# Idle products ahead of the feed-forward part, own PSUM banks for its two halves of rows, and one strided copy for each half

## The chip, the cores and the metric

One core of one Trainium2 chip. The metric is the device time of one execution in microseconds (us). A profile's own times count from the first instruction and end some 1.8 us lower than the device time.

Each run is labelled fast or slow; for one core, slow means no more than "over 1.5% above the fastest run of the same kernel". In the traces TensorE's granted clock is 0.50 or 1.00 and changes only at edges of a grid of 3.41 us. I compare all runs of the same rounds, and give the ratio of the fast ones beside that.

## The reference

A gated linear attention (RWKV) over `[4, 8, 768, 48]`, then a mixture of experts with soft slots over its 3072 rows of 384:

```python
# attention, for each step t
cur = u * k_t (x) v_t;  y_t = r_t . (state + cur);  state = w * state + k_t (x) v_t
# soft experts: 8 experts, 4 slots each, F = 1024
logits = x @ phi                                  # [3072, 32]
slot_input = softmax(logits, axis=0).T @ x        # [32, 384]
for e in range(8):
    slot_out[e] = relu(slot_input[e] @ w1[e]) @ w2[e]
out = softmax(logits, axis=1) @ slot_out
```

## The kernel before

Twelve blocks of 256 rows go through attention and the routing sums; GpSimd meanwhile issues the loads of the experts' weights. Behind the loop come the last routing, the feed-forward part (32 slots, all experts, on column strips of the array) and the output. The parts that matter:

```python
    hT = cst.tile([P, 2, nF, P], bf, name="hT")
    nc.gpsimd.memset(hT[:], 0.0)                      # at the start
    # ...
        ones_t = cst.tile([P, ES + 16], f32, name="ones_t")[:, 0:ES]
        nc.vector.tensor_reduce(ones_t, ident[:].rearrange("p (g t) -> p t g", g=G), ...)   # cut
        nc.vector.tensor_copy(idrep[:], ones_t[:, None, :].to_broadcast([P, G, ES]))
    # ...
        W_AT = [1] * 9 + [32] * 5                     # weight loads issued after each block
        for n in range(nS):                           # nS = 12; cut to the order on TensorE
            att(n, 0); disp(n - 2, s_now); trans(n + 1, "rr"); att(n, 1)
            # ... y_open, inter, state; trans(n + 1, "kk"); rowsum; xt(n - 1); intra(n); lg(n - 1)
            load_w(W_AT[n])
        disp(nS - 2, s_now)
        last_routing(nS - 1)
        disp(nS - 1, s_now)
        # ... csum_r, unsiT on DVE
        lexp_t(nG - 1)                                # transpose on PE, copy on ACT
        rowsum(nG - 1)
    # ...
        def up(x):
            h_p = ffn_ps.tile([P, 2, F // 2], f32, name=f"h_p{x}")      # both halves, one tile
            h_s[x] = ffn.tile([P, 2, F // 2], bf, name="h_s")
            for fh in range(2):
                for mi in range(nM):
                    for c in range(XE):
                        nc.tensor.matmul(h_p[c * ES:(c + 1) * ES, fh, :], unsiT[:, mi, :],
                                         w1_all[:, x * XE + c, mi, fh * (F // 2):(fh + 1) * (F // 2)],
                                         start=(mi == 0), stop=(mi == nM - 1), tile_position=(0, c * ES),
                                         skip_group_check=True)
                # relu of this half: DVE for fh == 0, ACT for fh == 1
        def turn(x):
            # per half: four transposes into hT_p, then
                for c in range(XE):
                    o = c * ES + (x * XE + c) * Spe
                    eng = nc.vector.tensor_copy if c % 2 == 0 else nc.scalar.copy
                    eng(hT[:, x, sl, o:o + Spe], hT_p[:, :, o:o + Spe])
        up(0); up(1); turn(0); down(0); turn(1); down(1)
```

The softmax here doesn't subtract the row's maximum and nothing guards it: scores larger than these inputs give would overflow.

## Time and profile before

| | value |
|---|---|
| time, median of 4 runs | 143.39 us (142.93 to 144.71) |
| span of the profile | 141.2 us |
| PE, DVE, ACT, POOL busy | 69%, 72%, 55%, 56% |
| feed-forward part in the profile | 109.74 to 123.99 us |
| last packet of the weight queue | 116.66 us |

The page's row of the granted TensorE clock, one digit for each fortieth of the span (3.5 us), 9 for full and 5 for half:

```profile
PEclk9999999995996986999757978999655555995555
```

From slice 29 (counted from 0) the row reads 5: the clock is at half through the last routing and the up products, and full only for slices 34 and 35.

### The profile page before, as it was taken

Reading aid. Unit: us, or ns where it says so; the run is one execution under the profiler, and the core shown is the slowest. Engines: PE = TensorE matmul, PEld = TensorE weight load, DVE = VectorE, ACT = ScalarE, POOL = GpSimd, SP = SyncE. Lnnn points to the kernel's source line nnn. Section 1 sums busy time; section 2 is a strip of 40 time slices with the busy share of each in tenths; the row PEclk is TensorE's granted clock in tenths of the full one; section 3 lists DMA queues with packets and bytes.
Section 4 is the critical chain, followed back from the end, with each engine's and each line's share of the span. In section 5 each row is a group of like instructions: output and inputs, shape, how many; then the busy total and the mean of one; then the engine's idle time right before and its main releaser. Section 6 shows DMA issues by size and latency. Waiting matters only on the chain.

```text
span 141.2 us, 4091 instructions
## 1 busy us (share of the span) xinstructions
PE 97.7 (69%) x1715; PEld 67.9 (48%) x1715; DVE 101.7 (72%) x198; ACT 77.5 (55%) x136; POOL 79.0 (56%) x63
## 2 busy tenths in 40 slices
PE   0826496769759869685898857786866679959200
PEld 0325284658557556564577645664454226623000
DVE  7899998999796888889986878989633211169510
ACT  4839466676775584949583766858033013128510
POOL 7309999999998749595895939995000000000000
PEclk9999999995996986999757978999655555995555
DMA  2999997999999999999999999999999990009994
GB/s 34 323 325 322 325 324 167 188 287 235 265 216 276 223 232 253 203 202 289 211 263 235 208 299 186 194 197 210 204 205 203 204 148 0 5 0 358 411 404 168
DMA packets 51351, 31.78 MB, mean 225 GB/s; under 512 B 38386, under 2 KB 46836, under 8 KB 51332
## 3 DMA queue, kind: packets, MB, share of 16 engines
q0 software_dynamic: 11600, 12.63, 54.2%
q1 hardware_dynamic: 39316, 18.88, 46.7%
q8 instruction: 13, 0.21, 0.5%
q10 hardware_dynamic: 416, 0.00, 0.2%
q14 instruction: 6, 0.05, 0.1%
HBM read 39.38 MB, written 4.72 MB: 312 GB/s over the span
## 4 chain that ended last, share of the span: by engine, by line
PE 37%; DVE 32%; ACT 17%; DMA 5%; issue 4%; POOL 0%; DVEq 0%; ACTq 0%; POOLq 0%
DVE at_s L292 14%; PE at_p L287 7%; ACT t_kk L272 5%; DMA out_dram<-o_s 5%; ACT v_bf L219 4%; PE h_p L535 4%; DVE k_l L238 4%; PE so_p L561 4%; ACT xt_s L381 4%; PE s_p L332 3%; PE t_p L269 3%; PE xl_p L379 3%; ACT rp L232 2%; PE xl_p L416 2%; PE y_p L314 2%
## 5 line engine op out<-in xcount | busy, mean ns | idle before, releaser
L292 DVE TENSOR_TENSOR at_s<-at_p,mask 128x512 bf16<-128x512 f32 x48 | 30.9, 685 | 7.9 <-PE at_p L287 7.8
L209 POOL TENSOR_TENSOR rr<-r_l,W_n 128x768 bf16<-128x768 f32 x11 | 20.0, 1817 | 16.3 <-DMA r_l<-in_r_dram 16.2
L211 POOL TENSOR_TENSOR kk<-k_l,W_k 128x768 bf16<-128x768 f32 x11 | 20.6, 1875 | 0.4 <-PE s_p L332 0.4
L212 POOL TENSOR_TENSOR k_l<-k_l,u_rep 128x768 f32<-128x768 f32 x11 | 20.0, 1814 | 0.9
L232 ACT COPY rp<-r_l 128x384 f32<-128x384 f32 x23 | 11.2, 486 | 14.4 <-DVE k_l L238 12.7
L287 PE MATMUL at_p<-t_rr,t_kk 64*64 64x128 bf16 x384 | 14.7, 250 | 6.1 <-DVE at_s L292 4.8
L272 ACT COPY t_rr<-t_p 128x1024 bf16<-128x1024 bf16 x11 | 11.1, 1012 | 9.7 <-PE t_p L269 9.6
L171 POOL DMA_DIRECT2D w_all<-in_moe_w_dram x19 | 15.6, 831 | 1.3 <-DMA w_all<-in_moe_w_dram 1.3
L287 PEld LDWEIGHTS <-t_kk 64*64 64x64 bf16 x384 | 9.0, 121 | 9.6 <-issue 7.7
L272 ACT COPY t_kk<-t_p 128x1024 bf16<-128x1024 bf16 x12 | 12.1, 1005 | 2.8 <-PE t_p L269 2.6
L238 DVE TENSOR_TENSOR k_l<-k_l,rp 128x384 f32<-128x384 f32 x23 | 12.6, 549 | 0.8
L341 DVE TENSOR_TENSOR st<-s_p,wm 128x384 bf16<-128x384 f32 x20 | 11.0, 552 | 1.9 <-PE s_p L332 1.9
L332 PE MATMUL s_p<-v_bf,kk 64*128 64x96 bf16 x160 | 12.4, 229 | 0.0
L256 DVE TENSOR_TENSOR dv<-v_bf,rp 128x768 bf16<-128x768 bf16 x12 | 11.4, 953 | 1.2
L249 DVE TENSOR_REDUCE rp<-k_l 128x16 f32<-128x768 f32 x12 | 11.5, 958 | 0.3
L332 PEld LDWEIGHTS <-kk 64*128 64x128 bf16 x160 | 9.0, 107 | 5.3 <-issue 5.3
L269 PE MATMUL t_p<-ident,kk 128*128 128x128 bf16 x96 | 9.1, 251 | 3.1 <-DVE kk L205 3.1
L381 ACT COPY xt_s<-xl_p 128x768 bf16<-128x768 bf16 x11 | 8.8, 800 | 3.6 <-PE xl_p L379 3.6
L365 ACT CAST x_t<-y_p 128x768 bf16<-128x768 f32 x11 | 8.9, 806 | 2.8 <-PE y_p L354 2.8
L219 ACT CAST v_bf<-v_l 128x768 bf16<-128x768 f32 x12 | 9.9, 828 | 0.0
L314 PE MATMUL y_p<-st,t_rr 128*128 128x96 bf16 x80 | 8.2, 236 | 2.3 <-DVE st L341 2.3
L598 ACT ACTIVATE o_s<-o_p,rsum_r 128x384 f32<-128x384 f32 x12 | 6.4, 585 | 5.9 <-PE o_p L590 3.7
(103 smaller groups left out, 180.9 us busy)
## 6 DMA issues: line engine op xcount, KB each, us to landing
w_all<-in_moe_w_dram POOLq DMA_DIRECT2D x15, 768.0 KB, 9.6
k_l<-in_k_dram SPq DMA_DIRECT2D x12, 384.0 KB, 10.2
r_l<-in_r_dram SPq DMA_DIRECT2D x12, 384.0 KB, 9.2
v_l<-in_v_dram SPq DMA_DIRECT2D x12, 384.0 KB, 9.2
out_dram<-o_s SPq DMA_DIRECT2D x11, 384.0 KB, 4.1
w_all<-in_moe_w_dram POOLq DMA_DIRECT2D x4, 192.0 KB, 19.6
out_dram<-o_s SPq DMA_DIRECT2D x2, 192.0 KB, 1.9
phi_f<-in_moe_phi_dram POOLq DMA_DIRECT2D x1, 48.0 KB, 4.7
```

The costliest lines, as they stand in the source:

```text
L171: nc.gpsimd.dma_start(out=dst, in_=src)
L209: nc.gpsimd.tensor_mul(rr[:, :, :, 0:D], jh(r_l), W_n[:])
L211: nc.gpsimd.tensor_mul(kk[:, :, :, 0:D], jh(k_l), W_k[:])
L212: nc.gpsimd.tensor_mul(ku, ku, u_b)
L219: nc.scalar.copy(v_bf[:], jh(loads[n][2]))
L232: nc.scalar.copy(rp[:], jh(loads[n][0])[:, j, :, :])
L238: nc.vector.tensor_mul(s["ku"][:, j, :, :], s["ku"][:, j, :, :], s["rps"][j][:])
L272: nc.scalar.copy(t_s[:], t_p[:])
L287: nc.tensor.matmul(at_p[a][g * HF:(g + 1) * HF, q, :], kT[sl, q, g, j, :], rT[sl, q, g, :, :].rearrange("p j c -> p (j c)"), start=True, s ...
L292: nc.vector.tensor_mul(s["at"][:, a, j, :, :], at_p[a][:], mask[:, j, None, :].to_broadcast([P, nP, P]))
L332: nc.tensor.matmul(s_p[:, q * D2:(q + 1) * D2], s["kk"][sl, j, 2 * q:2 * q + 2, :].rearrange("p h d -> p (h d)"), s["v"][sl, j, 2 * q:2 * ...
L381: nc.scalar.copy(xt_s[:], xl_p[:, 0:XW])
```

## The change

Its intent: keep the array's clock up into the feed-forward part with products whose result nobody reads, and take away the waits inside that part. It also moves hT's memset from the start to a late block and builds `idrep` in another way, since one copy for a half now needs each expert's slots at the same offset of its strip. The diff, cut (...):

```diff
     hT = cst.tile([P, 2, nF, P], bf, name="hT")
-    nc.gpsimd.memset(hT[:], 0.0)
...
-    unsiT = cst.tile([P, nM, ES], bf, name="unsiT")
+    unsiT = cst.tile([P, nM, 2, ES], bf, name="unsiT")
...
-        ones_t = cst.tile([P, ES + 16], f32, name="ones_t")[:, 0:ES]
-        nc.vector.tensor_reduce(ones_t, ident[:].rearrange("p (g t) -> p t g", g=G),
-                                axis=mybir.AxisListType.X, op=ALU.add)
-        nc.vector.tensor_copy(idrep[:], ones_t[:, None, :].to_broadcast([P, G, ES]))
+        nc.vector.memset(idrep[:], 0.0)
+        for c in range(XE):
+            nc.vector.tensor_copy(idrep[c * ES:(c + 1) * ES, :, c * Spe:ES], ...)
...
+        def fill(count):
+            pad = ps.tile([P, H, D], f32, name="pad", tag="rp")
+            for _ in range(count):
+                nc.tensor.matmul(pad[:].rearrange("p h d -> p (h d)"), ident[:], w1_all[:, 0, 0, 0:Dm],
+                                 start=True, stop=True, skip_group_check=True)
...
             trans(n + 1, "rr")
+            if n == nS - 1:
+                fill(2)
...
             trans(n + 1, "kk")
+            if n == nS - 1:
+                fill(2)
...
             load_w(W_AT[n])
+            if n == nS - 3:
+                nc.gpsimd.memset(hT[:], 0.0)
+        fill(2)
         disp(nS - 2, s_now)
         last_routing(nS - 1)          # with fill(2) between its transposes and its products
         disp(nS - 1, s_now)
+        fill(4)
...
-            h_p = ffn_ps.tile([P, 2, F // 2], f32, name=f"h_p{x}")
+            h_p = [ffn_ps.tile([P, F // 2], f32, name=f"h_p{x}{fh}") for fh in range(2)]
...
-                for c in range(XE):
-                    o = c * ES + (x * XE + c) * Spe
-                    sl = slice(fh * (nF // 2), (fh + 1) * (nF // 2))
-                    eng = nc.vector.tensor_copy if c % 2 == 0 else nc.scalar.copy
-                    eng(hT[:, x, sl, o:o + Spe], hT_p[:, :, o:o + Spe])
+                own = slice(x * XE * Spe, x * XE * Spe + Spe)
+                eng = nc.vector.tensor_copy if fh == 0 else nc.scalar.copy
+                eng(hT[:, x, sl, :].rearrange("p f (c t) -> p f c t", c=XE)[:, :, :, own],
+                    hT_p[:].rearrange("p f (c t) -> p f c t", c=XE)[:, :, :, own])
```

I call the two tiles of `h_p` "own banks": no trace shows the banks. The fills come to twelve products of 128x128 by 384 columns. Two of the expectations below say fourteen; that was a miscount of mine.

## The prediction

> **What bounds the kernel now.** I read the chain of work that ended last first, because no engine is busy throughout (DVE 72%, PE 69% of a 141.2 us span). Its lines behind the loop:

> ```profile
> 109.74 1.49 PE h_p L535 x12
> 111.26 0.70 DVE h_s L540
> 112.00 2.77 PE h_p L535 x24
> 114.80 0.70 DVE h_s L540
> 115.55 1.47 PE h_p L535 x12
> 117.02 0.97 PE hT_p L550 x8
> 117.99 2.84 PE so_p L561 x32
> 120.82 0.55 PE hT_p L550 x8
> 121.41 2.56 PE so_p L561 x31
> ```

> The feed-forward part runs from 109.74 to 123.99: 14.25 us, one engine after the other. Twice TensorE stops for the relu of the first half of rows, though the next product needs only the other half: both halves lie in one tile. Two equal batches of 32 down products take 2.84 and 2.56 us, yet the second has 16 steps (a group of three strips, then one) and the first 8. The clock explains that. I found its edges by narrow windows; they lie 3.41 us apart, so I read windows on that grid (columns: length, busy PE, PEld, DVE, ACT, POOL, then granted clock, DMA share, GB/s):

> ```profile
> 92.99:96.41 3.42, 3.05 (x72) 2.40 (x72) 3.30 (x6) 2.42 (x5) 3.42 (x5) 1.00 1.09 196
> 96.41:99.82 3.41, 1.50 (x49) 1.23 (x46) 3.21 (x6) 1.92 (x4) 0.96 (x2) 1.00 1.11 210
> 99.82:103.23 3.41, 2.88 (x39) 1.76 (x28) 1.94 (x4) 0.27 (x1) 0.00 (x0) 0.50 1.30 203
> ...
> 110.06:113.47 3.41, 2.62 (x28) 1.00 (x24) 0.69 (x1) 0.00 (x0) 0.00 (x0) 0.50 1.31 201
> 113.47:116.89 3.42, 2.63 (x26) 0.65 (x16) 0.69 (x1) 0.60 (x1) 0.00 (x0) 0.50 0.82 125
> 116.89:120.30 3.41, 3.41 (x39) 2.64 (x39) 0.57 (x4) 1.19 (x5) 0.00 (x0) 0.50 0.02 5
> 120.30:123.71 3.41, 3.37 (x50) 1.92 (x42) 0.57 (x4) 0.59 (x4) 0.00 (x0) 1.00 0.00 0
> ```

> A window with 1.50 us of PE work cost the clock; 2.62 and 2.63 did not bring it back; 3.41 did. Over the whole trace a full clock fell after windows of 1.45 to 2.20 us and mostly stayed from 2.19 up; a half clock rose after 3.32 us or more and not after 3.22. So keeping needs about 65% and regaining about 97%.

> Last I read the timeline of the start, because the diff moves a memset from there:

> ```profile
> 2.08 2.70 DVE L115 TENSOR_SCALAR mask<-col_f,row 128x128 bf16<-128x128 f32 x2
> 2.80 1.82 POOL L126 MEMSET hT<- 128x2048 bf16 x1
> ...
> 10.39 1.89 POOL L209 TENSOR_TENSOR rr<-r_l,W_n 128x768 bf16<-128x768 f32 x1 [5.77 <-DMA r_l<-in_r_dram]
> 10.54 2.56 DVE L207 TENSOR_TENSOR k_l<-k_l,u_rep 128x768 f32<-128x768 f32 x1
> ...
> 12.25 2.52 POOL L211 TENSOR_TENSOR kk<-k_l,W_k 128x768 bf16<-128x768 f32 x1
> ```

> Two mask instructions of 128 columns end at 4.78, just behind the memset's end at 4.62. The product at 10.54 takes 2.56 us where its neighbours of 768 columns take 0.95; it ends 0.8 us behind GpSimd's product, which started 0.15 us earlier. Both DVE delays are on the chain.

> [...]

> **The change part by part.**

> (1) hT's memset leaves the start (not the headline, but I give it weight). The masks [...] end near 3.1, 1.65 us earlier. The DVE queue reaches u_rep at 6.2 instead of 7.8, but u_rep needs a product that PE ends at 6.71: 6.75, a gain of 1.05. The idrep work there was two instructions; it becomes five. With DVE starts some 0.15 us apart I put its cost at +0.2, so kk starts at 7.97 instead of 8.80, and the disputed product at 9.71 instead of 10.54. Now DVE is ahead of GpSimd, whose operand lands at 10.39: the product takes 0.95, ends at 10.66, and what followed at 13.20 starts near 10.7. TensorE's operands through ACT shift by 0.83 only, so the first masking at 15.12 comes near 12.7. GpSimd's k times u for the next block, done at 16.65, would end near 16.1, and DVE's product that needs it (18.38) can't start earlier: that leaves 2.2 us. Later blocks have 3 to 6 us between GpSimd and its reader, so 2.2 us should live through the loop. At its new place, behind the last weight issue at 98.64, the memset has until about 117: free.

> (2) Own banks for the halves: the two gaps vanish, 111.22 to 112.00 and 114.77 to 115.55, 0.79 each, together 1.6 us. PE's h_p work at half clock is then 12 steps of 512 columns at 0.427 = 5.1 us.

> (3) One copy for each half instead of four small ones that alternated between DVE and ACT: 16 become 4. The small ones took 0.17 us each with some 0.05 between, but ran beside the down products; only about 0.3 us of the first batch was exposed (2.84 against 8 steps of 0.32 = 2.56). Gain 0.3, less near 0.1 of new waiting. The reciprocal product doubles to 192 columns: +0.1, hidden behind the row sums.

> (4) The clock. A continuous feed-forward part at half clock is 5.1 up + 0.9 turn + 2.6 down + 0.9 turn + 5.1 down = 14.6 us; at full clock 7.3, and 7.5 with short waits. Without gaps it regains the clock by itself at the first edge behind a filled window: 3.1 to 6.5 us in, mean 4.8 (counting 0.3 of row-sum work directly ahead). Total 7.5 + 4.8/2 = 9.9 instead of 14.25: 4.35 us gained, which holds (2) and (3).

> (5) The fills, if the clock has already fallen. One costs what an equal product (L327) takes in the chain: 0.16 at full, 0.32 at half. Before the second att: mostly in a gap, 0 to 0.3. Before the row sums: 0.64 with a wait for DVE behind it that stays; +0.35. Before the dispatch: in a gap of 1.02, nothing. In the last routing: +0.27. Four ahead of the last Lexp transpose: 1.28 of PE time ahead of the transpose, ACT copy and row sums, which queue in front of the up products; less what h_p waited for the reciprocal in its old shared tile, +1.05. Sum 1.7 us later.

> Sum at half clock on entry: 2.2 + 4.35 - 1.7 = 4.85 us, thus 138.2. If the fills hold the clock, they cost some 0.3 in all and the feed-forward part lasts 7.5; but the last expert's weights land in pieces up to 116.66 (my sum over the software queue's packets; the window 116.89:120.30 shows 5 GB/s), and the last group needs them. So the end of the down products can't come much before 117, against 123.99: 7 us, thus 136.1.

> **The rivals.** (a) The fills keep the clock. For: one added at 98.7 lies in the poor window. Against: 1.50 + 0.32 is still under 2.2 us, and some 3.4 us window always finds this trough. I give 30%: 136. (b) The clock is down, fills only cost, the gapless part regains it: 70%, 138.2, with 0.9 either way from the phase. (c) The start gains nothing, because DVE still comes behind GpSimd at 10.39 or the loop waits for loads: 15%, adds 2.2 in either case, 140.3 for (b). For: the DMA queues are near full throughout. Against: loop chain pieces are DVE, ACT and PE, with POOL 0%. (d) Weight landings become the bound: only together with (a), a floor of 136.

> **Range and chances.** 0.7 x 138.2 + 0.3 x 136.1 = 137.6, plus 0.15 x 2.2 = 137.9 us. Phase gives 0.9, the loop's own throttled windows (six of half clock, some 0.6 us each by comparing block times of 7.2 and 8.4 to 9 us) another 1: 80% between 135.7 and 140.2. Faster by over 2% means under 140.2: 0.88; within 2%: 0.11; slower: 0.01.

> **What would show it.** Masks ending near 3.1 and the k times u product at 0.95 us; the first masking near 12.7; the last block's first masking near 96 instead of 98.26. No relu between the batches of h_p. The feed-forward part near 10 us at half clock on entry, or near 8 with PEclk at 1.00 before it. If the start is unmoved, step (1) is wrong; if the up products run at half clock to their end, the fills were only cost; if the last down group waits for DMA, (d) is at work. A clock that never rises in the feed-forward part would make the whole prediction wrong, near 142.

## The result, and the profile after

The changed kernel took 138.09 us at the median of 4 runs (135.43 to 139.65), against 143.39. The ratio of fast runs is 0.9475, interval 0.9341 to 0.9609: faster. (Ratios here are the mean time of one kernel's fast runs over that of the other's of the same rounds, so not quite the ratio of the medians.) Two later calls ran it again: all 16 runs lie between 134.83 and 139.87, mean 137.34.

The first profile fell on a run of 139.48, in the upper part of the spread. Its row of the clock, and its chain behind the routing (start, length, engine, tile, line):

```profile
PEclk9999999999855699869757977999755557999755
```

```profile
110.27 5.21 PE h_p L552 x48
115.49 0.34 PE hT_p L567 x4
115.92 0.20 DVE hT L571
116.17 1.48 PE so_p L578 x32
117.65 0.34 PE hT_p L567 x4
118.02 0.20 DVE hT L571
118.27 2.16 PE so_p L578 x32
```

The row has 5 from slice 29 again (counted from 0); it rises in slice 33, is full in slices 34 to 36 and falls in 37. All 48 up products are one piece; no relu stands between them. The part lasts 10.18 us, from 110.27 to the cast at 120.45, where it lasted 14.25. But it *begins* 0.53 us later than before, although the loop had come 1.39 us earlier to its last block (first masking at 96.87 against 98.26): the fills cost 1.9 us here. Its windows on the clock's grid show that they bought nothing in this run (length, PE busy, PEld, DVE, ACT, POOL, clock, DMA share, GB/s):

```profile
94.80:98.21 3.41, 1.55 (x38) 0.91 (x38) 2.94 (x6) 1.87 (x4) 0.85 (x2) 1.00 1.11 207
98.21:101.63 3.42, 3.42 (x35) 1.74 (x34) 1.98 (x4) 0.27 (x1) 2.38 (x2) 0.50 1.22 203
101.63:105.04 3.41, 3.06 (x55) 2.33 (x55) 0.74 (x2) 0.99 (x2) 0.00 (x0) 0.50 1.31 203
105.04:108.45 3.41, 2.87 (x34) 2.00 (x33) 1.12 (x4) 1.20 (x5) 0.00 (x0) 0.50 1.32 205
108.45:111.87 3.42, 2.71 (x24) 1.15 (x26) 0.79 (x4) 0.27 (x1) 0.00 (x0) 0.50 1.31 202
111.87:115.28 3.41, 3.41 (x36) 1.25 (x28) 1.30 (x2) 0.60 (x1) 0.00 (x0) 0.50 1.18 181
```

The clock fell at 98.21 and rose only at 115.28, 5.0 us into the feed-forward part. The second line is the surprise: PE is busy for the whole window and the clock stays at half. By the prediction's rule (97% busy regains it) it had to rise at 101.63.

The same kernel in a fast run, traced with the experiments (135.63 us, from e11):

```profile
99.04:102.46 3.42, 3.07 (x28) 1.94 (x26) 1.21 (x3) 0.00 (x0) 0.07 (x1) 0.50 1.31 203
102.46:105.87 3.41, 3.04 (x60) 2.22 (x58) 1.13 (x3) 1.40 (x3) 0.00 (x0) 0.50 1.32 204
105.87:109.28 3.41, 2.47 (x33) 1.50 (x35) 1.25 (x5) 1.11 (x4) 0.00 (x0) 1.00 1.31 204
```

```profile
108.86 2.77 PE h_p L552 x48
112.32 1.49 PE so_p L578 x32
114.41 2.16 PE so_p L578 x32
```

Here a window with 3.04 us of PE work brought the clock back at 105.87, 3 us ahead of the up products, which then take 2.77 instead of 5.21; the whole part lasts 7.74 us. A third trace (e4, 134.83 us) had the clock full from 94.0 on and never lost it before the output. So this kernel ran in all three ways: held, regained ahead of the feed-forward part, regained inside it.

The start, which answers to the last fence of the prediction:

```profile
2.07 0.75 DVE L115 TENSOR_SCALAR mask<-col_f,row 128x128 bf16<-128x128 f32 x2
7.48 0.76 DVE L193 COPY idrep<-ident 32x128 bf16<-32x128 bf16 x4
10.02 0.95 DVE L207 TENSOR_TENSOR k_l<-k_l,u_rep 128x768 f32<-128x768 f32 x1
10.46 2.17 POOL L209 TENSOR_TENSOR rr<-r_l,W_n 128x768 bf16<-128x768 f32 x1 [7.66 <-DMA r_l<-in_r_dram]
13.02 1.29 DVE L292 TENSOR_TENSOR at_s<-at_p,mask 128x512 bf16<-128x512 f32 x2
```

The masks end at 2.82: 0.75 us for the two, where they took 2.70. The product with u starts 0.44 us ahead of GpSimd's and takes 0.95 us; before, it started 0.15 us behind and took 2.56. Now GpSimd's product is the longer one (2.17 us, with a median of 1.82 for its eleven of this form). The prediction takes the order of the two starts for the cause; these two traces show one pair each and do not isolate it.

### What the clock answers to

The busy time failed as a measure, so I counted the work. From the timelines of eleven traces (before, changed, e1 to e6, e9 to e11) I took each 3.41 us window on the grid, and summed for all products in it: count x columns x (rows x columns of the tile) / (128 x 128). That is columns of the full array. A product of 384 columns on the full array takes 0.16 us at full clock in these traces (0.66 for four fills in e4 and e11), so a window has room for about 8,190 of them at full clock and half of that at half (an estimate from these two numbers). Over 306 windows that end before 118 us, one limit tells whether the next window has the full clock, whatever the present clock: about 3,000 columns. Limits of 2,950 to 3,050 misjudge 13 to 17 of the 306. A single limit on busy time misjudges 90 at best, and two limits, one for each clock, 39. The rows count too: with columns x width of the tile alone the best limit misjudges 39, with columns alone 75. Transposes are in the sum: they run at both clocks (128 columns start 107 ns apart at half and 56 ns at full, in the changed kernel's profile), and without them the best limit misjudges 79. It is a rule read off these traces, not a mechanism that I tested alone; window edges and missing matmul records make it inexact.

It fits most of the lines above. The fully busy window of the changed kernel held 2,757 columns, many of its products being tiles of 64x64 or of few columns; the three behind it 2,908, 3,039 and 2,576; the one that regained the clock 3,953. (The 3,039 is one of the misjudged, if the limit is 3,000. A recount that splits a product between two windows by its time gives 2,782, 2,931, 3,076, 2,707 and 4,139 for these five, so one window's count is good to some 25 to 190 columns. The number of misjudged windows stays at 13.) In the fast run, 2,585 did not and 3,211 did. A fill is 384 columns, an eighth of the limit, for 0.16 us at full or 0.32 at half clock (e4's four take 0.66, two in e5 at half clock 0.64): dense work for its time. Before the change the windows from 99.82 to 116.89 held 2,081, 2,363, 1,384, 2,789 and 2,597.

### The profile page after: what moved, and what is told of

It reads as the page before. It is cut to its first block, busy times and chain, and to the rows that moved or that the text cites.

```text
span 137.7 us, 4106 instructions
## 1 busy us (share of the span) xinstructions
PE 98.7 (72%) x1727; PEld 67.7 (49%) x1727; DVE 98.0 (71%) x195; ACT 76.8 (56%) x130; POOL 78.6 (57%) x63
## 4 chain that ended last, share of the span: by engine, by line
PE 39%; DVE 26%; ACT 19%; issue 5%; DMA 5%; POOL 0%; DVEq 0%; ACTq 0%; POOLq 0%
DVE at_s L292 14%; PE at_p L287 7%; ACT t_kk L272 5%; DMA out_dram<-o_s 5%; ACT v_bf L219 4%; DVE k_l L238 4%; PE h_p L552 4%; PE t_p L269 4%; PE s_p L332 4%; ACT xt_s L381 3%; PE xl_p L379 3%; PE so_p L578 3%; ACT rp L232 2%; PE y_p L314 2%; DVE dv L256 2%
## 5 line engine op out<-in xcount | busy, mean ns | idle before, releaser
L209 POOL TENSOR_TENSOR rr<-r_l,W_n 128x768 bf16<-128x768 f32 x11 | 20.3, 1847 | 17.7 <-DMA r_l<-in_r_dram 17.6
L211 POOL TENSOR_TENSOR kk<-k_l,W_k 128x768 bf16<-128x768 f32 x11 | 20.0, 1814 | 0.0
L354 PE MATMUL y_p<-v_bf,at_s 64*128 64x48 bf16 x384 | 9.6, 192 | 0.0
```

Of the source, the lines that this page charges most:

```text
L209: nc.gpsimd.tensor_mul(rr[:, :, :, 0:D], jh(r_l), W_n[:])
L211: nc.gpsimd.tensor_mul(kk[:, :, :, 0:D], jh(k_l), W_k[:])
```

## The experiments

"Against before" is the difference of the means of all runs of the same rounds; with standard deviations of 0.4 to 2.1 us for one run, such a difference has a standard error of some 0.4 to 0.9 us. All gave the right result.

| run | kernel | mean (lowest to highest) | against before | ratio of fast runs |
|---|---|---|---|---|
| e1 | before, memset moved | 141.44 (139.23 to 144.00) | -1.3 | 0.9901 |
| e2 | changed, no fills | 137.24 (136.44 to 138.04) | -5.5 | 0.9744 |
| e3 | changed, memset at the start | 138.50 (136.82 to 141.75) | -4.2 | 0.9773 |
| e4 | changed | 137.57 (134.83 to 139.87) | -5.1 | 0.9604 |
| e5 | before, fills only | 138.87 (137.63 to 141.01) | -3.1 | 0.9809 |
| e6 | changed, no fills, shared tile | 140.36 (137.70 to 143.43) | -1.6 | 0.9792 |
| e7 | changed, no fills, weights early | 145.84 (143.18 to 147.91) | +3.9 | 1.0189 |
| e8 | changed, weights early | 145.74 (142.60 to 147.57) | +3.8 | 1.0142 |
| e9 | changed, shared tile | 138.08 (135.04 to 141.35) | -3.5 | none (one fast run) |
| e10 | changed, no fills | 137.66 (136.96 to 138.09) | -3.9 | 0.9738 |
| e11 | changed | 136.79 (135.41 to 138.19) | -4.8 | 0.9633 |
| e12 | changed, no fills, sixth block's weights | 140.18 (137.06 to 141.86) | -1.4 | 0.9739 |

The theory at the outset was the prediction's: the start gives 2 us, the gapless part regains the clock by itself, and the fills cost what they don't repay unless they keep the clock. The rivals: the fills are what brings the clock; the start is lost again; the weights set the end.

### e1: only the memset

```diff
-    nc.gpsimd.memset(hT[:], 0.0)
...
             load_w(W_AT[n])
+            if n == nS - 3:
+                nc.gpsimd.memset(hT[:], 0.0)
```

> The kernel before with one thing changed: hT's memset moves behind the last weight issue. Theory (start): the masks end near 2.8 us instead of 4.78, the k-times-u product takes 0.95 us, the first masking starts near 12.9 instead of 15.12, and the whole run is 1.4 to 2.2 us shorter than before (ratio 0.985 to 0.990). Rival (the loop waits for loads, or the clock gives it back): the start moves in the trace but the time stays within 0.5 us of before.

Measured: first masking at 12.48 us, ratio 0.9901 with interval 0.9812 to 0.999 (unclear at 2%), mean 1.3 us below before. The start moved by 2.6 us and about half reached the end. It leans to the theory; the size is not sharp.

### e2 and e10: no fills

```diff
         def fill(count):
+            return
```

> The changed kernel with all 14 idle products left out. Theory (fills only cost while the clock is down, the gapless feed-forward part regains it by itself): the feed-forward part begins near 108.5 in the trace, 1.5 to 1.9 us earlier than with fills, still regains the clock 3 to 7 us in, and the time is 1 to 2 us shorter than the changed kernel's median of 138.1, thus near 136.5. Rival (the fills keep or regain the clock in part of the runs): slower than the changed kernel by 0.5 us or more, without its fast runs of 135.4.

> The changed kernel without fills once more, for more runs. Theory (with own banks and one copy for each half, the fills are worth nothing on average: they cost what they win, and the landing of the last weights near 117 caps the best cases): mean within 0.7 us of the changed kernel in the same rounds, and a smaller spread (no runs under 136, none over 138.5). Rival (fills still help by 1 us or more, and the earlier runs were chance): mean 1 us or more above the changed kernel.

Measured: means 137.24 and 137.66, against 137.57 and 136.79 for the changed kernel in the same rounds (e4, e11): the fills are worth -0.3 to +0.9 us, 0.3 on average, inside the noise. All twelve runs lie between 136.44 and 138.09: a spread of 1.7 us, against 5.0 with the fills. The fast runs alone favour the fills by 1.4 and 1.1 points of ratio (some 2 and 1.5 us). I put that down to the spread: all twelve runs without fills count as fast, but only two of six (e4) and four of six (e11) with them, so these are picked from the lower end. That is an argument and not an experiment; by the fast runs alone the fills would be worth having. As the theory said, the feed-forward part starts early (107.13 in e2) and regains the clock by itself, 2.7 us in (3.3 in e10). What neither theory of e2 had: it then waits. The down products of e2 (start, length, ..., idle before, and what ended it):

```profile
113.96 1.48 PE L579 MATMUL so_p<-w_all,hT 128*32 128x384 bf16 x26
115.86 0.48 PE L579 MATMUL so_p<-w_all,hT 128*32 128x384 bf16 x2 [0.42 <-DMA w_all<-in_moe_w_dram]
116.83 0.48 PE L579 MATMUL so_p<-w_all,hT 128*32 128x384 bf16 x2 [0.49 <-DMA w_all<-in_moe_w_dram]
118.04 0.48 PE L579 MATMUL so_p<-w_all,hT 128*32 128x384 bf16 x2 [0.72 <-DMA w_all<-in_moe_w_dram]
```

The last expert's four pieces of weights arrive one by one, the last packet at 117.57, and the products follow each. e10 waits once, for the last piece (0.21 us; last packet 118.2). This is the bound that the prediction gave only to the best case of the fills; both traces without fills and with own banks reach it. Whether it also makes the narrow spread is not shown.

The bound is not a fixed time. In the eleven traces with the loads as they were, the last packet ends between 114.9 (e4) and 118.3 us (e9), and always 30.4 to 32.1 us after GpSimd starts the last batch of weight loads behind the tenth block (83.5 us in e4, 86.0 in e2, 87.8 in e10). In e2 and e10 the chain of work that ended last runs from that start through GpSimd and the last load to the last down products. So a faster loop should move the bound too; that was not tested alone.

### e3: the memset back at the start

```diff
     hT = cst.tile([P, 2, nF, P], bf, name="hT")
+    nc.gpsimd.memset(hT[:], 0.0)
...
-            if n == nS - 3:
-                nc.gpsimd.memset(hT[:], 0.0)
```

> The changed kernel with hT's memset put back at the start. Theory (start): masks blocked again until about 4.7 us, and 1.4 to 2.2 us slower than the changed kernel. Rival (the start is worth nothing by the end): same time as the changed kernel within 0.5 us.

Measured: first masking at 15.65 us, mean 0.9 us above e4, with a standard error of 1.1: no more than a hint. (The ratios of the fast runs differ by 1.7 points, some 2.5 us, but e4 has only two fast runs.) Pooled over the traces it is clearer. The first masking of the last block comes at 98.26, 98.33 and 98.92 where the memset is at the start (before, e5, e3), and at a mean of 96.87 (94.64 to 97.95) in the eight traces where it is moved and the loads are as they were (changed, e1, e2, e4, e6, e9, e10, e11). So 1.6 of 2.1 us live through the loop. At the end the means leave about 1 us (e1, e3), which with errors of 0.8 and 1.1 us can't be told from 1.6.

### e4 and e11: the changed kernel again

> The changed kernel itself, unchanged, for its spread in the same rounds as the other three. Theory (the phase of the clock windows decides): times spread over 135.4 to 139.7 again, in no fixed order, longer where the mean granted clock is lower. Rival (two fixed states of the chip): two clusters with nothing between.

> The changed kernel itself, beside the other three of this call. Theory: mean 137 to 138.3, wide spread of some 135 to 140 as the clock windows fall. Rival (a slow or fast state of one chip): all six runs at one end of that.

Measured: 134.83 to 139.87 and 135.41 to 138.19, with no gap between clusters, as expected. Their traces, described above, differ in where the clock fell and rose (full from 94.0 on in e4, back at 105.87 in e11); that this makes the spread was not tested.

### e5: the fills alone

> The kernel before plus the 14 idle products at the places of the change, nothing else. Theory (the fills are a cost of 1 to 1.7 us while the clock is down, and the two relu waits in the shared tile still keep every window under 97%): 0.5 to 1.7 us slower than before, ratio 1.003 to 1.012. Rival (the fills are what keeps or regains the clock): 1.5 us or more faster than before, with the clock at 1.00 in the up products of the trace.

The diff is the `fill` lines of the change, put into the kernel before. Measured: 3.1 us faster than before (ratio of the fast runs 0.9809, interval 0.9742 to 0.9877, so clear of noise on both counts). **Here my theory fell** and its rival won: the fills are no mere cost. The windows of e5, again on the grid:

```profile
103.40:106.81 3.41, 2.85 (x53) 2.10 (x53) 0.69 (x2) 1.40 (x3) 0.00 (x0) 0.50 1.32 204
106.81:110.23 3.42, 3.25 (x35) 2.13 (x34) 1.54 (x5) 0.79 (x3) 0.00 (x0) 0.50 1.32 204
110.23:113.64 3.41, 1.91 (x30) 0.93 (x32) 0.88 (x2) 0.27 (x1) 0.00 (x0) 1.00 1.32 203
```

The window with the last routing's fills and the four behind the dispatch holds 3,584 columns (the one before it 2,904), and the clock rises at 110.23, ahead of the up products at 111.38. The relu waits in the shared tile are still there (0.79 us each), and the window that contains them (1.91 us busy, some 2,980 columns) just kept the clock.

### e6 and e9: the shared tile, without and with fills

```diff
-            h_p = [ffn_ps.tile([P, F // 2], f32, name=f"h_p{x}{fh}") for fh in range(2)]
+            h_p = ffn_ps.tile([P, 2, F // 2], f32, name=f"h_p{x}")
```

(Cut: the lines that index `h_p` follow, and e6 also leaves the fills out.)

> The changed kernel without fills and with the two halves of rows in one tile again. Theory (own banks give 1.6 us directly and let the clock rise some 3 us earlier): 3 to 4 us slower than the same kernel with own banks (137.1), near 140.5; the two waits of 0.79 us are back in the chain and the clock rises only behind the up products. Rival (the landing of the last weights near 117 sets the end in any case): within 1.5 us of 137.1.

> The changed kernel with its fills, but the two halves of rows in one tile again: the fourth corner of fills by tiles. Theory (fills and own banks are two ways to the same thing, a clock that rises at or before the feed-forward part; either one alone gives most of it): between 137.5 and 139, thus at most 1.3 us slower than the changed kernel in the same rounds, though the same edit without fills cost 3 us. Rival (the two gains add): 3 us slower than the changed kernel, near 140.7.

Measured, as differences to before in the same rounds:

| | no fills | fills |
|---|---|---|
| shared tile | -1.6 (e6) | -3.5 (e9) |
| own banks | -5.5, -3.9 (e2, e10) | -5.1, -4.8 (e4, e11) |

By these means own banks are worth 2.3 to 3.9 us without fills (3.1 on average) and 1.3 to 1.6 with them; fills are worth 1.9 on the shared tile (3.1 in e5) and about nothing on own banks. Each seems to replace much of the other. The sizes are not settled: the error is near 1 us on each difference, and the fast runs say less (e6 has 0.9792 from two fast runs against 0.9744 and 0.9738 with own banks, 0.5 points; e9 has one fast run).

The traces show what goes with it. Without either, the up products of e6 pause twice:

```profile
105.27 1.47 PE L553 MATMUL h_p<-w_all,unsiT 128*32 128x512 bf16 x12 [0.51 <-DVE rsum_r L461]
107.53 2.75 PE L553 MATMUL h_p<-w_all,unsiT 128*32 128x512 bf16 x24 [0.79 <-DVE h_s L558]
111.07 1.47 PE L553 MATMUL h_p<-w_all,unsiT 128*32 128x512 bf16 x12 [0.79 <-DVE h_s L558]
```

The clock rises behind them, at 115.46; with fills and the shared tile (e9) it rises at 106.82, ahead of them. The other traces agree: in none of the seven without fills was the clock full when the up products began, and in five of the seven with fills it was (e3, e4, e5, e9, e11; not in the first profile and not in e8).

### e7, e8 and e12: weights issued earlier

If the last weights set the end, issue some earlier:

```diff
-        W_AT = [1] * 9 + [32] * 5
+        W_AT = [2, 2] + [1] * 7 + [32] * 5           # e7 (no fills), e8 (fills)
+        W_AT = [1] * 5 + [2] + [1] * 3 + [32] * 5    # e12 (no fills)
```

> The changed kernel without fills, and with two weight loads instead of one issued after each of the first two blocks, so that two fewer remain for the last batch. Theory (without fills the last expert's weights set the end, and the DMA queues have room between 21 and 28 us): the last landing moves from 117.6 to 112 to 115, no down product waits for DMA, time 134.5 to 135.5. Rival (the queues are full throughout and only the order changes, or later blocks wait for their loads): landing moves by under 1 us and the time stays at 137.

> The changed kernel with its fills, and with the same two weight loads earlier. Theory (with fills the start of the feed-forward part and the clock set the end in most runs, the landing only in the fast ones): median 0.3 to 1.2 us under the changed kernel's 138.0, fast runs down to 134 or below; slower than the kernel without fills with the same loads by 1 to 2 us. Rival (weights bind everywhere): down by as much as the kernel without fills, 2 us or more.

> The changed kernel without fills and with one more weight load, issued after the sixth block instead of in the last batch. GpSimd has 4 to 6 us between its work and the reader there, and the queues moved 0.8 to 0.9 of their load between 54 and 84 us. Theory (the landing of the last weights caps this kernel): last landing near 114.5 to 116 instead of 117.6, time 1 to 2 us under the kernel without fills in the same rounds, near 135.5. Rival (as in the two failed runs with early weights, the key, receptance and value loads are what is pushed back): later blocks start later and the time is the same or longer.

Measured: 8 to 9 us slower than the same kernels without the edit in e7 and e8, 2.5 us slower in e12 (against e10; its two fast runs equal e10's, with ratios of 0.9739 and 0.9738). The theory fell each time: nothing became faster and the last packet came later, as the rival had it or worse. GpSimd's view of e7 shows it: in the changed kernel the wait for r_l has no entry over 7.7 us (the one at the start), here it waits 10.5 us in mid-loop:

```profile
53.52 1.79 POOL L209 TENSOR_TENSOR rr<-r_l,W_n 128x768 bf16<-128x768 f32 x1 [10.52 <-DMA r_l<-in_r_dram]
```

The weights took their place from the loop's own loads: a load of r_l that is issued at 26.57 us in both traces lands at 37.59 in the changed kernel and at 53.43 here. The second masking of the sixth block moved from 52.51 to 57.01, and the last weight packet still landed at 120.02 (118.97 in e8, 119.05 in e12). At none of these three places did an earlier load bring the last landing forward (117.57 in e2, 118.2 in e10); others were not tried. So the bound stands, and no version here beats the changed kernel: without fills it is equal on average (137.45 of 12 runs against 137.34 of 16) and steadier.

## Why the prediction was right or wrong

The predicted 137.9 us met a median of 138.09 (reckoned from 143.08, the median of the three runs known then). Not every step behind it held.

What stays open: whether fills that reach 3,000 columns in *each* window from the last block on would hold the clock in all runs, and whether that is worth more than the landing of the weights (115 to 118 us here) allows. Whether starting the last batch of loads sooner by a faster loop would help is untested, and so is the single copy for each half by itself.

## What to carry to other kernels

Two cures for one illness need not add: take away the waits inside a stage first, and ask whether padding still buys anything beyond a wider spread. If you pad for the clock, count array columns for each window, not busy time (here one limit on columns misjudges 13 to 17 of 306 windows, one on busy time 90), and put the padding where the engine would have waited. Before shortening the end of a kernel, look up when its last load lands and what starts it: ahead of that time the work that needs the load can't end, and here the landing moved with the loop.
